# Another bank for the second layer behind a switch, and case numbers loaded one block ahead

## The chip, the cores and the metric

The kernel runs on one core of a Trainium2 chip. The metric is the time of one execution in microseconds (us) on the device, as the median of several runs. PE is the matrix engine (TensorE), PEld its weight loads, DVE the vector engine, ACT the scalar engine, POOL GpSimd and SP the engine that starts most transfers. A name with a q behind it (PEldq, DVEq, ACTq, POOLq) is the instruction queue of that engine, where register, branch and semaphore instructions run.

## The reference, cut to what matters

An attention with a window and some global rows makes 8 x 544 = 4352 rows of 512 numbers. Each row then goes through one of 8 experts, chosen by a gate that may keep the expert of the row before:

```python
def _moe_ref(x, w_gate, w_local, w1, w2):
    ...
            e = fresh_e if s == 0 or local_gate[b, s] < 0.5 else prev_e
            ...
            h = np.maximum(x[b, s] @ w1[e], 0.0)
            out[b, s] = p[e] * (h @ w2[e])
```

w1 is 8 x 512 x 1024 and w2 is 8 x 1024 x 512, all in 32-bit floats. How many rows each expert gets is known only when the kernel runs.

## The kernel before, in words

Until about 290 us the attention fills PE, and the rows that it makes go to a table `xs` in device memory. Then follow the experts, in blocks of up to 512 rows of one expert. Each matrix product is taken as three, with every operand split into a rounded high part and a low rest (`hi`, `lo`; `XH`, `XL` for the rows; `HH`, `HL` for the hidden layer).

`run` goes through `block(i)`:

- i = 0 to 2 are "early" blocks of 256 rows (`early`), during which the lists of the rows are still being made.
- i = 3 to 10 are "rem" blocks, one per expert, of a number of rows that is known only at run time. The text counts them as rem 1 to rem 8. A `tc.Switch` over `NCASE` = 34 cases picks the code ("arm") by a case number, `self.cv[k]`, a register on each engine, loaded from the tile `cnd` by `bound`. Case 0 is `half` (few rows, with the operands of the first layer exchanged), the others are `part` with another width of the row tile.
- i = 11 and up are "full" blocks of 256 rows under nested `tc.If`; three of them run with this input.

The chip has 8 banks of PSUM, `ps[0]` to `ps[7]`, each 128 x 512 numbers. In a `part`, the first layer makes 8 column blocks (`fc` = 0 to 7). Each is 12 matmuls into one bank (`mm1`, L1282), and the banks are taken in the order 2, 3, 6, 1, 7, 2, 3, 6. ACT reads a bank through a relu into `HH` (L1284), and DVE makes `HL` (L1287). Then comes the second layer (`mm2`, L1295; `thin`, L1301), 24 matmuls for 128 rows into a bank: ps0 or ps1 (`self.py.t`), or ps7 for the last part of a rem block.

The 128 rows with the number 2 (`REM`), the middle rows, are in every arm, and their second layer comes once behind the switch, where the arms join: `close(i, REM)`. `close` first stores ps7, then runs 24 matmuls, then stores that bank too. `store` is an ACT instruction that scales the bank into a tile `y` (L1313) and an indirect transfer on POOL that scatters `y` to the output (L1314).

Just ahead of `close`, `hint(i + 1)` loads the case number of the next block (`bound`, a TENSOR_LOAD of L1495 on each engine) and gives each engine the hint where the next switch will go (L1501: a few register instructions and a BRANCH_PREFETCH_HINT). For the first rem block this stands in `early(2)`, at `fc == 4` of the second layer.

Around this run three streams of preparation. Weights: SP loads raw tiles, ACT rounds them (`split`, L1174), and DVE makes the rest (L1184). Rows: POOL gathers the rows of block i + 2 (`gather`, L1215, four transfers per rem block). PE turns the rows of block i + 1 (`xpose`, L1236), and ACT and DVE copy the bank (L1238, L1239). In a `part` the four turns lie between second-layer matmuls, and the gather is issued behind the last. In `half` the turns and the gather stand at the end of the arm, where PE has little else to do.

The order on each engine is that of the code. A tile is guarded by semaphores that the framework sets from what uses it. Where a switch's arms join, the waits behind it count from the end of whichever arm ran, so one wait stands for all arms, and each arm is padded to the same counts.

## Time and profile before

| | us |
|---|---|
| median of three runs (lowest, highest) | 681.4 (680.08, 683.91) |
| profiled execution | 683.3 |
| its span | 681.6 |
| PE busy in it | 653.2 (96%) |
| DVE busy | 432.4 (63%) |
| ACT busy | 342.0 (50%) |
| POOL busy | 189.5 (28%) |

The mean granted clock of PE is 0.998. The profiled execution is 1.9 us above the median of the runs, and its span leaves out 1.7 us around it.

A row of the timeline has the start, the length, the engine, the line and operation, the tile written, the tile read, and the count of instructions that were put together; in brackets stands how long the engine was idle before it, and what ended that ("issue" means that no wait shows). Tiles bear the name of the buffer as it was allotted, so a piece of a weight may be called `wp`, `xh`, `hh` or `xa`.

The widths of the first layer's matmuls tell which arm ran: rem 1 has 456 columns, rem 2 is `half`, then 352, 440, 344, 288, 440 and 408 columns in rem 3 to rem 8. Their first layers begin at 321.8, 365.5, 382.4, 417.8, 459.3, 494.9, 524.5 and 566.0 us; the first full block begins at 605.0 us.

### The profile page before, as it was taken

What the parts mean: (1) busy time and instruction counts of PE and PEld (TensorE: products, weight loads), DVE (VectorE), ACT (ScalarE), POOL (GpSimd) and SP (SyncE); (2) the same over time, 40 slices, a digit from 0 to 9 for tenths busy, and PEclk for the clock granted to TensorE, in tenths of its full rate; (3) what the DMA queues carried; (4) which work ended last, traced back from release to release, by engine and by line L of the source; (5) the groups of instructions that cost most, each with busy time, mean ns of one, the idle gap of its engine ahead of it and who ended that gap; (6) DMA issues with size and microseconds to landing.
All of it is one profiled execution on the core that took longest, in us unless ns stands there. A gap on an engine that the chain in (4) does not pass through costs nothing.

```text
span 681.6 us, 18538 instructions
## 1 busy us (share of the span) xinstructions
PE 653.2 (96%) x7285; PEld 554.9 (81%) x7285; DVE 432.4 (63%) x1099; ACT 342.0 (50%) x612; POOL 189.5 (28%) x321
## 2 busy tenths in 40 slices
PE   8999999999999899998999899999999999999996
PEld 7778778777677787886988887989798989898994
DVE  7878788788887677987424653535353525355663
ACT  4555556554555674643426634344444435255563
POOL 7634344243334301031121303030303020212012
PEclk9999999999999999999999999999999999999999
DMA  8956958866857497766636566437474636355683
GB/s 326 406 211 251 346 202 321 317 236 238 296 200 288 144 330 276 262 201 205 250 116 223 196 235 204 155 117 224 139 226 115 212 117 202 131 184 185 225 269 107
DMA packets 42882, 151.42 MB, mean 222 GB/s; under 512 B 7838, under 2 KB 9118, under 8 KB 38561
## 3 DMA queue, kind: packets, MB, share of 16 engines
q1 hardware_dynamic: 35536, 126.92, 52.5%
q0 software_dynamic: 6832, 21.90, 9.9%
q8 instruction: 77, 1.26, 0.7%
q14 instruction: 149, 1.21, 0.6%
q10 hardware_dynamic: 288, 0.13, 0.1%
HBM read 130.55 MB, written 19.16 MB: 220 GB/s over the span
## 4 chain that ended last, share of the span: by engine, by line
PE 56%; DVE 5%; issue 2%; ACT 1%; POOL 1%; DVEq 0%; POOLq 0%; ACTq 0%
PE ps L1282 27%; PE ps L1295 23%; PE ps L1236 2%; PE ps L1301 2%; DVE wq L1184 1%; DVE wp L1184 1%; PE ps L1421 1%; DVE xT L1003 0%; ACT wp L1238 0%; POOL out_dram L1314 0%; DVE xT L1001 0%; PE ps L1011 0%; ACT wp L1174 0%; DVE o L917 0%; DVE xl L1239 0%
## 5 line engine op out<-in xcount | busy, mean ns | idle before, releaser
L1295 PE MATMUL ps<-wp,wq 128*128 128x512 f32 x444 | 111.3, 398 | 2.8 <-ACT wp L1238 2.8
L1282 PE MATMUL ps<-wp,wp 128*128 128x256 f32 (+6 forms) x672 | 108.0, 320 | 1.5 <-issue 1.5
L1282 PEld LDWEIGHTS ps<-wp,wp 128*128 128x128 f32 x672 | 103.2, 188 | 5.9 <-issue 2.7
L1215 POOL DMA_INDIRECT xa<-xs,idx x42 | 41.7, 992 | 209.6 <-PE ps L1295 103.1
L1295 PEld LDWEIGHTS ps<-wp,wq 128*128 128x128 f32 x444 | 81.5, 188 | 20.0 <-ACT wp L1238 3.1
L1287 DVE SCALAR_TENSOR_TENSOR wq<-ps,wq 128x384 fp32r<-128x384 f32 (+4 forms) x112 | 42.8, 412 | 64.6 <-ACT wq L1284 56.7
L1314 POOL DMA_INDIRECT out_dram<-y,tk x39 | 43.3, 1109 | 124.9 <-ACT y L1313 80.2
L194 POOL TENSOR_SCALAR_AFFINE_SELECT qbd<-raw 64x512 f32<-64x512 f32 x62 | 44.5, 718 | 116.9 <-PE ps L247 96.3
L1184 DVE TENSOR_TENSOR wp<-raw,wp 128x1024 fp32r<-128x1024 f32 x47 | 56.8, 1217 | 24.6 <-ACT wp L1174 18.3
L1284 ACT ACTIVATE wq<-ps 128x256 fp32r<-128x256 f32 (+6 forms) x80 | 36.6, 465 | 71.3 <-PE ps L1282 63.9
L247 PE MATMUL ps<-kx,qbd 128*64 128x128 f32 x1024 | 67.3, 274 | 1.5 <-issue 1.0
L258 ACT ACTIVATE pe<-pe 128x512 f32<-128x512 f32 x64 | 40.7, 636 | 44.0 <-DVE pe L254 44.0
L247 PEld LDWEIGHTS ps<-kx,qbd 128*64 128x64 f32 x1024 | 58.4, 138 | 2.3 <-issue 1.2
L1313 ACT ACTIVATE y<-ps,pp 128x512 f32<-128x512 f32 x35 | 24.2, 691 | 70.1 <-PE ps L1295 49.7
L252 DVE TENSOR_REDUCE mx<-ps 128x4 f32<-128x512 f32 x64 | 43.8, 685 | 23.8 <-PE ps L247 23.6
L1174 ACT CAST wp<-raw 128x1024 fp32r<-128x1024 f32 x49 | 50.5, 1048 | 1.3 <-ACT hh L1284 0.5
L1238 ACT CAST wp<-ps 128x512 fp32r<-128x512 f32 x40 | 23.4, 590 | 47.4 <-PE ps L1236 46.1
L1239 DVE TENSOR_TENSOR wp<-ps,wp 128x512 fp32r<-128x512 f32 x40 | 27.5, 691 | 29.3 <-ACT wp L1238 29.1
L254 DVE TENSOR_TENSOR pe<-ps,mx 128x512 f32<-128x512 f32 x64 | 44.0, 687 | 1.6
L280 PEld LDWEIGHTS ps<-v,pt 128*32 128x32 f32 x2048 | 32.9, 110 | 14.0 <-issue 8.3
L194 POOL TENSOR_SCALAR_AFFINE_SELECT kx<-raw 128x384 f32<-128x384 f32 (+3 forms) x127 | 42.9, 372 | 2.7 <-DMA raw<-in_qk_dram 0.5
L280 PE MATMUL ps<-v,pt 128*32 128x65 f32 x2048 | 41.4, 222 | 2.1 <-DVE xa L288 0.7
(302 smaller groups left out, 1185.6 us busy)
## 6 DMA issues: line engine op xcount, KB each, us to landing
raw<-in_w_dram SPq DMA_DIRECT2D x78, 512.0 KB, 3.7
v<-in_vw_dram SPq DMA_DIRECT2D x32, 1040.0 KB, 7.5
raw<-in_qk_dram SPq DMA_DIRECT2D x32, 528.0 KB, 8.0
xa<-in_w_dram SPq DMA_DIRECT2D x26, 512.0 KB, 4.3
xT<-in_w_dram SPq DMA_DIRECT2D x20, 512.0 KB, 5.5
xs<-xa SPq DMA_DIRECT2D x8, 1056.0 KB, 6.1
qgb<-in_qg_dram SPq DMA_DIRECT2D x8, 128.0 KB, 4.5
xa<-xs,idx POOLq DMA_INDIRECT x42
```

The lines of the kernel that those rows point to most:

```text
L194: self.nc.gpsimd.affine_select(out=out, in_=in_, pattern=pat, compare_op=ALU.is_ge, fill=0.0, base=0, channel_multiplier=0)
L247: nc.tensor.matmul(sp[64 * t2:64 * t2 + 64, t], qbd[:, w], kf[:, f:f + P], start=False, stop=True, skip_group_check=True)
L252: nc.vector.tensor_reduce(out=mx, in_=st["sp"], axis=AX.X, op=ALU.max)
L254: nc.vector.tensor_tensor(out=st["pe"][:, 4 * hb:4 * hb + 4], in0=st["sp"], in1=mx.broadcast_to([P, 4, P]), op=ALU.subtract)
L280: nc.tensor.matmul(o[32 * w4:32 * w4 + 32, g, h], pt[:, 2 * g + w4 // 2, w4 % 2, h, :], v[:, w, h * (D + 1):(h + 1) * (D + 1)], start=True ...
L1174: nc.scalar.copy(out=hi, in_=raw)
L1184: (nc.gpsimd if pool else nc.vector).tensor_tensor(out=lo, in0=raw, in1=hi.bitcast(F32), op=ALU.subtract)
L1215: self.nc.gpsimd.indirect_dma_start(out=self.xr[j] if k == "early" else self.xr4[:, j], out_offset=None, in_=src, in_offset=bass.IndirectO ...
L1282: nc.tensor.matmul(ph, a[:, dc, fs], b_[:, dc, n0:n1], start=(n == 0), stop=(n == 11))
L1287: nc.vector.scalar_tensor_tensor(out=o[:, fc, c:c + b_ - a], in0=ph[:, a - n0:b_ - n0], scalar=0.0, in1=hh[:, fc, a:b_].bitcast(F32), op0= ...
L1295: nc.tensor.matmul(py, a[:, fc, js], b_[:, fs], start=(fc == 0 and k == 0), stop=(fc == 7 and k == 2))
L1314: sc = nc.gpsimd.indirect_dma_start(out=self.out, out_offset=bass.IndirectOffsetOnAxis(ap=tk[rows, js], axis=0), in_=y[rows], in_offset=No ...
```

## The change

Two edits.

The bank. For a rem block `close` uses `ps[6]` in place of ps0 (`self.py.t[0]`). In `half` the four banks of the first layer are taken as 2, 3, 1, 6 in place of 2, 3, 6, 1, and the last turn goes into `ps[0]` in place of `ps[6]`.

The case number. A new function `ahead(i + 2)` stands right behind `hint(i + 1)`, in `early(2)` and behind each switch. It loads the case number of the block after next, so that at the next hint the number is in the register and no load stands ahead of it. Behind the hint for rem 8 it loads the number for the `If` of the full blocks, which was loaded ahead of the first `If`. In `early(2)` stand two loads now, one ahead of the hint and one behind it.

```diff
@@ early
                 self.hint(i + 1)
+                self.ahead(i + 2)
@@ half
-            ph = ps[(2, 3, 6, 1)[k]][:, 0:256]
+            ph = ps[(2, 3, 1, 6)[k]][:, 0:256]
...
-        self.xpose(i + 1, 3, ps[6])
+        self.xpose(i + 1, 3, ps[0])
@@ close
-        py = self.py.t[j % 2]
+        py = self.ps[6] if self.kind(i) == "rem" else self.py.t[j % 2]
@@ new, behind bound
+    def ahead(self, i):
+        if self.kind(i) == "rem":
+            self.bound(1 + i - NX, NCASE - 1)
+        else:
+            self.bound(0, NR)
@@ block, behind the switch
             self.hint(i + 1)
+            self.ahead(i + 2)
             self.close(i, REM)
```

The rows of PE where the arms of the first switch join, before. Names are tile and number of use: `cnd_298` is the tile of case numbers, `ps0_63` bank 0, `wp6` a piece of the second layer's weights, `wq0` and `wq1` are `HH` and `HL`. `Activation_49` and `DVE_49` are the semaphores that ACT and DVE raise.

```order
L1625 UNCONDITIONAL_BRANCH
L1495 TENSOR_LOAD cnd_298
L1501 SWITCH_STRIDE
L1501 ISA
L1501 BRANCH_PREFETCH_HINT
L1295 MATMUL ps0_63<-wp6_4376,wq0_4378 128x512 [waits Activation_49]
L1295 MATMUL ps0_63<-wp6_4376,wq0_4378 128x512
L1295 MATMUL ps0_63<-wp6_4376,wq1_4379 128x512 [waits DVE_49]
```

The same place now (L1496 is the load, L1508 the hint):

```order
L1633 UNCONDITIONAL_BRANCH
L1508 SWITCH_STRIDE
L1508 ISA
L1508 BRANCH_PREFETCH_HINT
L1496 TENSOR_LOAD cnd_298
L1295 MATMUL ps6_69<-wp6_4376,wq0_4378 128x512 [waits DVE_49,Activation_49]
L1295 MATMUL ps6_69<-wp6_4376,wq0_4378 128x512
L1295 MATMUL ps6_69<-wp6_4376,wq1_4379 128x512
```

The load has changed places with the hint, the second layer writes bank 6, and its first matmul carries the wait for DVE that the third had; the other joins read alike.

The rows of PE in the first layer of a rem block, in the arm with 440 columns of the second switch, before: the second, third and fourth column block. `wp4` and `wp5` are the high and low rows, `hl` and `wp0` pieces of the weights.

```order
L1282 MATMUL ps3_66<-wp4_4273,hl_91 128x440 x8
L1282 MATMUL ps3_66<-wp5_4375,hl_91 128x440 x4
L1282 MATMUL ps6_69<-wp4_4273,wp0_100 128x440 x4
L1282 MATMUL ps6_69<-wp4_4273,wp0_100 128x440 [waits DVE_49]
L1282 MATMUL ps6_69<-wp4_4273,wp0_100 128x440 x3
L1282 MATMUL ps6_69<-wp5_4375,wp0_100 128x440 x4
```

And now:

```order
L1282 MATMUL ps3_66<-wp4_4273,hl_91 128x440 x8
L1282 MATMUL ps3_66<-wp5_4375,hl_91 128x440 x4
L1282 MATMUL ps6_69<-wp4_4273,wp0_100 128x440 [waits Activation_49]
L1282 MATMUL ps6_69<-wp4_4273,wp0_100 128x440 x3
L1282 MATMUL ps6_69<-wp4_4273,wp0_100 128x440 [waits DVE_49]
L1282 MATMUL ps6_69<-wp4_4273,wp0_100 128x440 x3
L1282 MATMUL ps6_69<-wp5_4375,wp0_100 128x440 x4
```

The third column block, which takes bank 6, now begins with a wait for ACT; what it waits for is the store (L1313) of the `close` before, which reads that bank.

## The prediction

> **What bounds the kernel now.** The first part of the page comes first:

> ```profile
> span 681.6 us, 18538 instructions
> PE 653.2 (96%) x7285; PEld 554.9 (81%) x7285; DVE 432.4 (63%) x1099; ACT 342.0 (50%) x612; POOL 189.5 (28%) x321
> L1295 PE MATMUL ps<-wp,wq 128*128 128x512 f32 x444 | 111.3, 398 | 2.8 <-ACT wp L1238 2.8
> L1282 PE MATMUL ps<-wp,wp 128*128 128x256 f32 (+6 forms) x672 | 108.0, 320 | 1.5 <-issue 1.5
> ```

> PE is busy 96% of the span. The change takes no matmul away and adds none, so it can only move PE's idle time. The waits of PE from 290 us on, where the experts run (total, times, longest):

> ```profile
> PE ps L1282 <- issue: 3.1, 2, 1.6
> PE ps L1295 <- ACT wp L1238: 2.8, 1, 2.8
> PE ps L1236 <- DVE wp L1239: 2.2, 1, 2.2
> PE ps L1282 <- DVE hl L1287: 1.6, 1, 1.6
> PE ps L1295 <- ACT wp L1174: 0.7, 1, 0.7
> ```

> Together 10.4 us. The first row is two switches, the second the join behind the half arm, the third early block 2. These three lie where the change works; all of them taken away would be 8.1 us, 1.2% of the time. What the change can add must be a new wait, so I went to the timeline at each join.

> **The join behind the half arm (rem 2).** Rows of the timeline of ACT, DVE, PE and POOL there:

> ```profile
> 373.22 1.07 ACT L1174 CAST hh<-raw 128x1024 fp32r<-128x1024 f32 x1
> ...
> 374.81 0.69 DVE L1239 TENSOR_TENSOR wp<-ps,wp 128x512 fp32r<-128x512 f32 x1 [0.52 <-ACT wp L1238]
> ...
> 375.59 1.10 ACT L1238 CAST wp<-ps 128x512 fp32r<-128x512 f32 x2
> ...
> 376.74 4.40 PE L1295 MATMUL ps<-wp,wq 128*128 128x512 f32 x18 [2.82 <-ACT wp L1238]
> ...
> 378.81 1.33 POOL L1215 DMA_INDIRECT xa<-xs,idx  x1 [11.16 <-PE ps L1295]
> ...
> 382.35 4.01 PE L1282 MATMUL ps<-wp,hh 128*128 128x352 f32 x24
> ...
> 384.94 0.69 ACT L1313 ACTIVATE y<-ps,pp 128x512 f32<-128x512 f32 x1 [2.93 <-DMA xa<-xs,idx]
> ...
> 386.19 4.01 PE L1282 MATMUL ps<-wp,hl 128*128 128x352 f32 x24
> ```

> Now the second layer waits for ACT's last two copies of turned rows, which end at 375.59 + 1.10 = 376.69. With bank 6 the count that it needs of DVE and ACT is an earlier one: by the order of the two engines' instructions, the subtraction at 374.81, which ends at 375.50, and the cast at 373.22, which has long ended. PE's last copy at 376.74 started 0.05 behind its release, so it would start at 375.55: 1.19 us earlier.

> The third column block of rem 3 stands at 386.19 and would come to 385.00. It takes bank 6 and now waits for the store that empties it: 384.94 + 0.69 = 385.63. That store doesn't move, as it waits for the gather issued at 378.81, 6.1 us before, which is on POOL and depends on the turns that the change leaves in place. With the same 0.05, PE starts at 385.68 instead of 386.19. Net -0.5 us of the 1.2. The price is between -1.2 (the store is done in time) and +0.6 (the second layer starts no earlier, the wait comes anyway); -0.5 is the value that the rows themselves give.

> **The other joins.** Every rem block and the first full block get the same new wait at the third column block, 24 matmuls behind the end of `close`. Behind rem 6:

> ```profile
> 524.49 14.65 PE L1282 MATMUL ps<-wp,wp 128*128 128x440 f32 x72
> ```

> ```profile
> 525.06 1.14 POOL L1215 DMA_INDIRECT xa<-xs,idx  x1 [0.30 <-issue]
> ...
> 531.54 0.69 ACT L1313 ACTIVATE y<-ps,pp 128x512 f32<-128x512 f32 x1 [4.77 <-issue]
> ```

> ```profile
> L1313 ACTq EVENT_SEMAPHORE  x5: 17/38/8808, 522.2 to 531.5; - x5
> ```

> The first row is PE in rem 7, the next two POOL's last gather and ACT's store, the fourth the store's waits in ACT's queue from 520 to 535 us (least, median and greatest, in ns). Rem 7 takes bank 6 at 524.49 + 24 x 14.65 / 72 = 529.37. ACT's store of the second layer stands in the queue for 8.8 us, behind the gather issued at 525.06, and ends at 531.54 + 0.69 = 532.23. Nobody waits for it before, as bank 0 isn't needed until the second layer of rem 7. Bank 6 is: PE would stop for 532.23 + 0.05 - 529.37 = 2.9 us. Nothing hides this; behind it PE is as full as before. It is zero if the gather lands 2.9 us earlier, and grows with each us that it lands later. I take 2.9.

> The other stores end in time. The closest is the first full block, PE and then ACT:

> ```profile
> 604.97 7.30 PE L1282 MATMUL ps<-wp,wp 128*128 128x256 f32 x60
> ```

> ```profile
> 605.22 0.69 ACT L1313 ACTIVATE y<-ps,pp 128x512 f32<-128x512 f32 x1 [1.04 <-issue]
> ```

> Bank 6 is wanted at 604.97 + 24 x 7.30 / 60 = 607.89, the store ends at 605.91: 2.0 us to spare, cost 0.

> **The hint without a load ahead of it.** The two gaps at switches (rem 4 and rem 6), and PE's queue at them: the compare and branch of the switch (L1625), and the load and the hint at the join:

> ```profile
> 417.83 1.06 PE L1282 MATMUL ps<-wp,xh 128*128 128x440 f32 x4 [1.59 <-issue]
> ...
> 494.86 6.61 PE L1282 MATMUL ps<-wp,wp 128*128 128x288 f32 x48 [1.53 <-issue]
> ```

> ```profile
> L1625 PEldq COMPARE_BRANCH x2: 303/2870/5438, 406.5 to 412.2; - x2
> ...
> L1495 PEldq TENSOR_LOAD <-cnd x1: 314/314/314, 406.8 to 406.8; - x1
> ...
> L1501 PEldq MOVE x3: 29/29/34, 407.3 to 407.6; - x3
> ...
> L1501 PEldq BRANCH_PREFETCH_HINT x1: 40/40/40, 407.8 to 407.8; - x1
> ...
> L1625 PEldq COMPARE_BRANCH x1: 5077/5077/5077, 489.5 to 489.5; - x1
> ```

> The branch at 412.2 takes 5.4 us until the arm's code is there; the queue of matmuls ahead of it covers all but 1.6 us. The hint is given 4.4 us ahead of the branch. The load begins at 406.8 and the hint's first move at 407.3. Without the load, the hint stands some 0.4 us earlier (0.31 of load, 0.1 behind it). If the code arrives a fixed time behind the hint, each gap shrinks by 0.4: -0.8 for both. The bounds are 0, where the fetch begins at the branch, and -3.1 (1.59 + 1.53), where an earlier hint gets ahead of other fetches. I take -0.8, nearest to the one row with a duration, the load. At the other switches PE shows no gap, so nothing is to be won there. The load now lies behind the hint, ahead of the second layer's first matmul in PE's queue; the queue runs ahead of PE (the hint of rem 4 at 407.8, the arm at 417.83), so this is hidden but behind the half arm, where PE waits for DVE longer than that.

> [...]

> **Early block 2.** Two loads now, one ahead of the hint and one behind. The chain of waits, DVE's load there, and PE's wait:

> ```profile
> 310.90 0.33 DVEq L1495
> ...
> 311.71 0.06 DVEq L1501
> 311.77 0.17 issue
> 311.94 0.61 DVE xT L1001
> ...
> 317.83 0.04 issue
> 317.88 0.66 PE ps L1236 x4
> ```

> The chain goes through DVE's queue: load, hint, then DVE's next instruction at 311.94, and DVE full until PE gets its bank at 317.88. A second load of 0.31 us behind the hint starts DVE 0.3 us later, and so PE. The bounds: 0 (the 0.17 and the 1.2 us instruction that runs on DVE then hide it) to +0.45 (load and the step behind it). I take +0.3. On PE, ACT and POOL the second load delays at most what ends before PE's wait of 2.2 us, which absorbs it. In all there are 9 loads per engine before and after; the one ahead of the first `If` moves to an earlier join, where PE's queue runs ahead, cost 0.

> **The sum.** +0.3 (early block 2) - 0.5 (half arm with rem 3) - 0.8 (two switches) + 2.9 (rem 7) = +1.9 us, on the profiled execution's 683.3. That execution stands 1.9 us above the median of the runs, 681.4; the change should add the same to the median: 683.3 us.

> **The rivals.**

> [...]

> *The hint does nothing.* The change then doesn't do what it says for the switch: 0 instead of -0.8, sum +2.7, 684.1 us. For it: the same 4.4 us that bought nothing visible.

> *The stores come in time.* The gathers land earlier than in this execution or the store waits for less than the trace shows, so neither rem 7 nor rem 3 stops: +0.3 - 1.2 - 0.8 = -1.7, 679.7 us. Against it: 6.1 and 6.5 us from issue to the store in two places. If both gaps went too: -4.0, 677.4 us.

> *The other side: the gathers land later.* The wait in rem 7 and that in rem 3 are both set by a gather, so each us by which gathers land later costs up to 2 us. The sum passes 3.4 us (0.5%, about what a measurement of this kernel can tell from no change) when they land 0.8 us later, 7.1 instead of 6.3. At 1.5 us later the sum is 1.9 + 3.0 = +4.9, 686.3 us. For it: the transfers are dense in that stretch. Windows: between, busy times of PE, PEld, DVE, ACT, POOL, granted clock, DMA share, GB/s:

> ```profile
> 373.90:376.70 2.80, 0.03 (x1) 0.00 (x0) 2.28 (x4) 2.80 (x6) 0.00 (x0) 1.00 0.03 13
> 376.70:382.50 5.80, 5.76 (x25) 4.77 (x26) 4.01 (x8) 5.31 (x6) 3.08 (x3) 1.00 0.67 224
> 529.40:532.30 2.90, 2.90 (x16) 2.73 (x15) 0.15 (x1) 0.69 (x1) 0.00 (x0) 1.00 0.87 282
> ```

> Against it: nothing in the change moves POOL's gathers or SP's transfers.

> *The clock falls in the new stall.* If the stop of 2.9 us in rem 7 brought the granted clock to half for as long again as it lasts, the work in these 2.9 us would lose half of them, 1.5 us: sum +3.4, 684.8 us. Against it: in 2.8 us of idle PE, the first two windows, the clock stayed at 1.00, and 2.9 is hardly more. [...]

> **How the numbers follow.** Forecast as summed, 0.45. Hint does nothing, 0.17. Hint overtakes, 0.13. Stores in time, 0.10, a third of it with both gaps gone. Gathers later, 0.11. Clock, 0.04. "Slower by over 0.5%" is the last two less the cases of a small delay, and the error of two medians (the three runs spread over 3.8 us): 0.14. "Faster" is the third of "stores in time" and that error: 0.06. The rest, 0.80, is within 0.5%. The likeliest case is 683.3 us; the range goes from "stores in time", 679.7, to "gathers later", 686.3.

> **What would show it.** In the profile after: PE L1282 waits for ACT y L1313 twice, 2.9 us at about 531 and 0.6 at about 385; PE L1295 behind the half arm is idle for 1.6 instead of 2.8, ended by DVE wp L1239; the issue gaps at rem 4 and rem 6 are 1.2 and 1.1; PE's wait in early block 2 is 2.5 instead of 2.2. Gaps of 1.6 again say that the hint has no part in the fetch, none at all that it leads it. No wait for L1313 would put my reading of the new wait wrong, and with it the sign of the sum.

## The result, and the profile after

The changed kernel takes 686.6 us (median of 9 runs, 685.5 to 689.5) against 681.9 us of the kernel before (9 runs beside them, 680.1 to 685.8). The ratio is 1.0067 with a 95% interval of 1.0047 to 1.0088: slower by 0.7%, 4.7 us, where 1.9 us were forecast. It lies 0.3 us above the forecast's range.

The profiled execution took 688.3 us. First part of its page:

```profile
span 686.6 us, 18548 instructions
PE 657.2 (96%) x7285; PEld 557.8 (81%) x7285; DVE 432.9 (63%) x1099; ACT 342.1 (50%) x612; POOL 190.9 (28%) x321
L1282 PE MATMUL ps<-wp,wp 128*128 128x256 f32 (+6 forms) x672 | 111.0, 326 | 3.6 <-ACT y L1313 3.5
```

The same 672 first-layer matmuls keep PE busy for 111.0 us instead of 108.0: 326 ns each instead of 320. Something has made equal work slower, besides the idle time. PE's waits from 290 us on:

```profile
PE ps L1282 <- ACT y L1313: 3.5, 1, 3.5
PE ps L1236 <- DVE wp L1239: 2.1, 1, 2.1
PE ps L1295 <- DVE wp L1239: 1.7, 1, 1.7
PE ps L1282 <- DVE hl L1287: 1.7, 1, 1.7
PE ps L1295 <- issue: 1.0, 1, 1.0
PE ps L1282 <- ACT wp L1174: 0.8, 1, 0.8
PE ps L1282 <- issue: 0.3, 1, 0.3
```

The first row is the new wait, once and not twice. The 2.8 us behind the half arm are 1.7, ended by DVE. The two gaps "issue" at switches are one of 0.3. PE's timeline and POOL's last gather and ACT's store in rem 7:

```profile
522.43 5.08 PE L1282 MATMUL ps<-wp,wp 128*128 128x440 f32 x24
...
531.02 4.40 PE L1282 MATMUL ps<-wp,wp 128*128 128x440 f32 x11 [3.51 <-ACT y L1313]
```

```profile
523.01 1.66 POOL L1215 DMA_INDIRECT xa<-xs,idx  x1 [0.30 <-issue]
...
530.28 0.69 ACT L1313 ACTIVATE y<-ps,pp 128x512 f32<-128x512 f32 x1 [5.42 <-issue]
```

PE stops after 24 matmuls until ACT has stored bank 6. Behind the stop 11 matmuls take 4.40 us, 0.40 each, where 24 took 5.08, 0.21 each. Windows around it, and around early block 2 (start and end, length, busy times of five engines, granted clock, DMA share, GB/s):

```profile
314.80:317.30 2.50, 0.37 (x2) 0.00 (x0) 2.46 (x5) 0.30 (x1) 0.00 (x0) 1.00 0.62 193
317.40:322.00 4.60, 4.60 (x31) 3.81 (x32) 2.16 (x6) 1.86 (x3) 0.24 (x1) 0.63 0.53 144
527.40:531.00 3.60, 0.11 (x1) 0.00 (x0) 0.15 (x1) 0.69 (x1) 0.00 (x0) 0.90 0.93 289
531.00:537.10 6.10, 6.08 (x17) 5.49 (x18) 2.15 (x4) 2.72 (x5) 1.00 (x1) 0.50 0.34 133
```

After the stop PE runs at half its clock for over 6 us. It also does for a while in early block 2, behind an idle time of only 2.1 us that stood in the profile before too (2.2 us) and left the clock at 1.00 there.

Both traces have the same 7285 matmuls, so the start of the same one in both tells where the time went:

| PE at | before | after | difference | step |
|---|---|---|---|---|
| third turn in early block 2 | 317.88 | 317.31 | -0.57 | differences ahead of the experts |
| first matmul of rem 1 | 321.81 | 322.84 | +1.03 | +1.60 half clock |
| second layer behind the half arm | 376.74 | 376.68 | -0.06 | -1.09 shorter wait |
| rem 3 | 382.35 | 383.24 | +0.89 | +0.95 branch of the switch ended late |
| rem 4 | 417.83 | 417.54 | -0.29 | -1.18 gap 1.59 to 0.32 |
| rem 6 | 494.86 | 492.89 | -1.98 | -1.69 gap 1.53 to 0 |
| rem 7 | 524.49 | 522.43 | -2.06 | -0.08 |
| third column block of rem 7 | 529.38 | 531.02 | +1.64 | +3.70 stop |
| sixth column block of rem 7 | 536.58 | 541.08 | +4.50 | +2.86 half clock |
| rem 8 | 565.97 | 570.70 | +4.73 | +0.23 |

Two of these rows, rem 4 and rem 6, are gains; whether they come from the change is a question for the experiments.

### The profile page after: what moved, and what is told of

Read it like the earlier page. It is cut to its first block, busy times and chain, and to the rows that moved or that the text cites. A ratio compares the mean times of both kernels' runs of the same rounds, so it can differ in the third digit from the quotient of the medians.

```text
span 686.6 us, 18548 instructions
## 1 busy us (share of the span) xinstructions
PE 657.2 (96%) x7285; PEld 557.8 (81%) x7285; DVE 432.9 (63%) x1099; ACT 342.1 (50%) x612; POOL 190.9 (28%) x321
## 4 chain that ended last, share of the span: by engine, by line
PE 51%; DVE 5%; DMA 3%; issue 3%; ACT 2%; POOL 1%; DVEq 0%; POOLq 0%; ACTq 0%
PE ps L1282 26%; PE ps L1295 19%; DMA out_dram<-y,tk 3%; PE ps L1236 2%; PE ps L1301 2%; DVE wq L1184 1%; DVE wp L1184 1%; ACT wp L1174 1%; POOL out_dram L1314 1%; POOL xa L1215 1%; PE ps L1011 0%; DVE xT L1003 0%; DVE xT L1001 0%; DVE o L917 0%; DVE xl L1239 0%
## 5 line engine op out<-in xcount | busy, mean ns | idle before, releaser
L1282 PE MATMUL ps<-wp,wp 128*128 128x256 f32 (+6 forms) x672 | 111.0, 326 | 3.6 <-ACT y L1313 3.5
L1295 PE MATMUL ps<-wp,wq 128*128 128x512 f32 x444 | 111.3, 397 | 1.7 <-DVE wp L1239 1.7
L1282 PEld LDWEIGHTS ps<-wp,wp 128*128 128x128 f32 x672 | 105.6, 192 | 8.5 <-ACT y L1313 3.9
L1215 POOL DMA_INDIRECT xa<-xs,idx x42 | 42.7, 1017 | 215.2 <-PE ps L1295 102.7
L1295 PEld LDWEIGHTS ps<-wp,wq 128*128 128x128 f32 x444 | 81.5, 188 | 18.9 <-ACT wp L1238 1.9
L1287 DVE SCALAR_TENSOR_TENSOR wq<-ps,wq 128x384 fp32r<-128x384 f32 (+4 forms) x112 | 42.9, 413 | 70.3 <-ACT wq L1284 63.9
L1313 ACT ACTIVATE y<-ps,pp 128x512 f32<-128x512 f32 x35 | 24.2, 691 | 67.8 <-PE ps L1295 54.4
L1174 ACT CAST wp<-raw 128x1024 fp32r<-128x1024 f32 x49 | 50.6, 1050 | 2.1 <-DVE wp L1184 1.3
L1238 ACT CAST wp<-ps 128x512 fp32r<-128x512 f32 x40 | 23.5, 590 | 47.7 <-PE ps L1236 46.3
L1239 DVE TENSOR_TENSOR wp<-ps,wp 128x512 fp32r<-128x512 f32 x40 | 27.5, 691 | 29.6 <-ACT wp L1238 29.4
```

Source lines behind the costliest of these rows:

```text
L1174: nc.scalar.copy(out=hi, in_=raw)
L1215: self.nc.gpsimd.indirect_dma_start(out=self.xr[j] if k == "early" else self.xr4[:, j], out_offset=None, in_=src, in_offset=bass.IndirectO ...
L1282: nc.tensor.matmul(ph, a[:, dc, fs], b_[:, dc, n0:n1], start=(n == 0), stop=(n == 11))
L1287: nc.vector.scalar_tensor_tensor(out=o[:, fc, c:c + b_ - a], in0=ph[:, a - n0:b_ - n0], scalar=0.0, in1=hh[:, fc, a:b_].bitcast(F32), op0= ...
L1295: nc.tensor.matmul(py, a[:, fc, js], b_[:, fs], start=(fc == 0 and k == 0), stop=(fc == 7 and k == 2))
```

## The experiments

All ran five rounds, interleaved with the kernel before; a ratio is to the kernel before on the same chip, with its 95% interval.

**The bank edit alone, the loads alone.** Without `ahead`:

```diff
-                self.ahead(i + 2)
-            self.ahead(i + 2)
```

> The bank edit alone: second layer into bank 6, the case number loaded ahead of the hint as before. Theory S (the stop in rem 7 and the half clock behind it cost 3.5 + 2.9 us, and the earlier hint pays 2.7 us back at the switches of rem 4 and rem 6): the stop stays and the payment goes, so slower than the changed kernel, 6 to 7 us above the kernel before (688 to 689), with gaps of about 1.5 us at those two switches and a granted clock near 0.5 for some microseconds behind the stop in rem 7. Rival L (the loss comes from the loads: two in early block 2, and shifted code): close to the kernel before, within 2 us.

Measured: 686.6 us, ratio 1.0061 (1.0038 to 1.0083). The other half of the change by itself, from the changed kernel:

```diff
-        py = self.ps[6] if self.kind(i) == "rem" else self.py.t[j % 2]
+        py = self.py.t[j % 2]
-            ph = ps[(2, 3, 1, 6)[k]][:, 0:256]
+            ph = ps[(2, 3, 6, 1)[k]][:, 0:256]
-        self.xpose(i + 1, 3, ps[0])
+        self.xpose(i + 1, 3, ps[6])
```

> The loads one block ahead alone, second layer in bank 0 as before. Theory S: no stop in rem 7, no fall of the clock there, gaps at rem 4 and rem 6 gone or under 0.5 us: 2 to 3 us faster than the kernel before (679 to 680). Rival L: 3 to 5 us slower than before, like the changed kernel. Rival N (the gaps vanished by chance in one execution): same as before within 1 us, with gaps of 1.5 us back.

Measured: 683.1 us, ratio 0.9997 (0.9981 to 1.0013). The loss is the bank edit's; the loads neither cost nor bring over 0.2%. Rival L falls, and so does the half of theory S by which the earlier hint pays 2.7 us back: without it the bank edit costs as much as with it. Rival N is borne out: the loads alone take the time of the kernel before. PE of the bank edit alone in rem 7, and the windows there:

```profile
530.51 11.41 PE L1282 MATMUL ps<-wp,wp 128*128 128x440 f32 x48 [3.63 <-ACT y L1313]
```

```profile
526.90:530.50 3.60, 0.00 (x0) 0.00 (x0) 0.15 (x1) 0.69 (x1) 0.00 (x0) 1.00 0.93 316
530.60:534.80 4.20, 4.20 (x14) 3.82 (x15) 1.41 (x3) 1.95 (x4) 1.00 (x1) 0.59 0.35 134
```

The stop is there again, and the clock falls again behind it, for about half as long.

**The stop taken away in two ways.** Bank 6 later in the first layer of every part:

```diff
-            self.mm1(..., self.ps[(2, 3, 6, 1, 7, 2, 3, 6)[fc]], few if thin else 0)
+            self.mm1(..., self.ps[(2, 3, 1, 7, 6, 2, 3, 1)[fc]], few if thin else 0)
```

> The changed kernel with the first layer of a part taking its banks in the order 2, 3, 1, 7, 6, 2, 3, 1, so that bank 6 is wanted 24 matmuls later. Theory S: the store has ended by then (4.9 us later at 440 columns against a stop of 3.5), no stop and no fall of the clock in rem 7: 6 us faster than the changed kernel, 680 to 681. Rival L: no better than the changed kernel, 686 to 687.

Measured: 680.2 us, ratio 0.9962 (0.9940 to 0.9985). Taking the stop away makes a kernel that is faster than before. The waits of PE in rem 7 (515 to 545 us) now have no store among them, but a smaller one of DVE, whose work follows ACT's. That the late store, which still holds ACT up, is the cause is argued, not shown:

```profile
PE ps L1282 <- DVE wq L1287: 0.9, 1, 0.9
```

The late order did more than take the stop away. In this trace the second layer behind the half arm runs on without any wait, where the changed kernel waits for 1.7 us, and in rem 3 PE waits for DVE for 1.6 us. This order wasn't run on the kernel before, so what it is worth by itself isn't known. PE behind the half arm:

```profile
375.26 4.37 PE L1295 MATMUL ps<-wp,wq 128*128 128x512 f32 x18
```

The other way is to let the store go earlier: an output tile of its own, here the attention's idle tile `gsb`.

```diff
+    def store(self, py, j, thin=False, y=None):
+        y = self.y() if y is None else y
...
+        self.store(py, j, y=self.yc if self.kind(i) == "rem" else None)
...
+    moe.yc = at.gsb
```

> The changed kernel with an output tile of its own for the store of the second layer behind the switch (an idle tile of the attention), so that ACT's store doesn't wait for transfers that share a semaphore with the gathers. If the store is late because of these transfers, it runs right behind the second layer (about 1 us behind the end of the arm), PE doesn't stop in rem 7, the clock stays at 1.00: 680 to 681. If the store is late because of ACT's own casts or of the bank, it stays late and the time stays at 686 to 687.

Measured: 684.9 us, ratio 1.0045 (1.0025 to 1.0065): neither value. The stop in rem 7 was gone, but this tile is also one that the half arm writes, and PE there waited for it:

```profile
372.30 0.71 PE L1410 MATMUL ps<-idf,gsb 128*128 128x128 f32 x4 [2.44 <-ACT gsb L1425]
```

So the time of this run doesn't tell what the store is worth. The same with a tile that the half arm doesn't touch (against the run just shown):

```diff
-    moe.yc = at.gsb
+    moe.yc = moe.xr[0][:, 0:DM]
```

> The changed kernel with an output tile of its own for the store behind the switch, this time one that the half arm doesn't write (the early blocks' row tile). If the store was late only because its output tile waits for transfers: no stop in rem 7 over 1 us, no fall of the clock there, and no wait in the half arm: 680 to 681. If not: 684 and above.

Measured: 680.5 us, ratio 0.9960 (0.9942 to 0.9978). ACT's row of the store, and the window of rem 7 in which PE had stopped:

```profile
523.87 0.69 ACT L1313 ACTIVATE xr<-ps,pp 128x512 f32<-128x512 f32 x1
```

```profile
526.00:532.00 6.00, 6.00 (x31) 5.63 (x30) 3.01 (x7) 3.51 (x6) 0.99 (x1) 1.00 0.89 297
```

The store runs right behind ACT's casts, 2.5 us behind the start of rem 7 (523.87 against 521.34), where it came 7.9 us behind it (530.28 against 522.43), and PE runs through. So the store was late because of its output tile, which comes from a ring whose last use lies in the arm: the wait for the transfers that emptied the ring ends only when the last gather has landed. By the profile that gather takes 7.0 us from issue to landing in the changed kernel (523.01 + 7.0 = 530.0) and 7.1 us with the bank edit alone (522.41 + 7.1 = 529.5); the store begins 0.3 us behind that in both, at 530.28 and 529.77. The profile's times for the last gather alone, in the changed kernel and with the bank edit alone:

```profile
DMA to landing us min/median/max: 7.0/7.0/7.0
DMA to landing us min/median/max: 7.1/7.1/7.1
```

The two remedies come to the same time within their intervals, 7 us under the changed kernel. Each has something of its own besides the stop: the late order the shorter wait behind the half arm, the own tile 0.2% on the kernel before (1.6 us, last experiment). With that taken off, 7.3 - 1.6 = 5.7 us are left for the stop and what follows it. That is the whole loss of 4.7 us, and probably more; the intervals, 1.2 to 1.4 us to each side, don't settle how much more.

**The clock's share.** PE is kept busy during the stop, in rem 7 alone:

```diff
+            if i == 9 and fc == 2:
+                w = self.wp[8 * i][0].rearrange("p (c f) -> p c f", c=4)
+                for m in range(12):
+                    self.nc.tensor.matmul(self.ps[0][:, 0:n1 - n0], w[:, 0, 0:P], x[0][:, 0, n0:n1], start=True, stop=True)
```

> The changed kernel, and in rem 7 twelve matmuls of no use (the arm's width, 440 columns here, into bank 0, which nobody reads) ahead of the third column block, where PE stops. They take 12 x 0.203 = 2.4 us of the stop of 3.5 us. Theory S: the third column block starts when it did (the store sets it), PE is idle for 1.1 us only, the clock stays at 1.00 in rem 7, and the time falls by what the clock cost there, 1.5 us per 3.4 us at half speed: 684 to 685.5. If the clock doesn't fall because of the idle time, or its fall costs nothing: 686.6 as the changed kernel.

Measured: 685.5 us, ratio 1.0032 (1.0014 to 1.0050). PE in rem 7, and the windows of the filled part, the idle part and behind them:

```profile
527.96 2.57 PE L1456 MATMUL ps<-wp,wp 128*128 128x440 f32 x12
532.31 9.88 PE L1282 MATMUL ps<-wp,wp 128*128 128x440 f32 x48 [1.78 <-ACT y L1313]
```

```profile
527.96:530.50 2.54, 2.54 (x13) 2.07 (x11) 0.00 (x0) 0.00 (x0) 0.00 (x0) 1.00 0.98 214
530.50:532.30 1.80, 0.03 (x1) 0.00 (x0) 0.15 (x1) 0.69 (x1) 0.00 (x0) 1.00 1.01 410
532.30:538.00 5.70, 5.69 (x28) 5.35 (x29) 2.95 (x6) 3.52 (x6) 1.00 (x1) 1.00 0.31 122
```

The useful work is held up for 4.35 us here (2.57 and 1.78), longer than the 3.51 of the changed kernel, and the clock stays at 1.00. The ratio falls by 0.0035, 2.4 us; the intervals of the two ratios overlap a little, so the size is rough. It goes the way of the clock: the mean granted clock was 0.9933 over 9 executions of the changed kernel and 0.9964 over 12 of this one, so (0.0031 x 686) / 0.5 = 4.3 us less at half speed, worth 2.1 us of work, less the 0.8 us by which the useful work is held up longer.

**Short idle times.** The same idea at the two places where PE always stands idle for about 2 us, on the kernel with the second own tile (`warm` writes matmuls of no use into a free bank):

```diff
+                if fc == XPM[2]:
+                    self.warm(i, self.ps[2], 7)
                 self.xpose(i + 1, XPM.index(fc))
...
+        self.warm(i, self.ps[1], 5)
         self.scals(i + 1)
```

> The changed kernel with the output tile of its own, and matmuls of no use where PE stands idle for about 2 us: seven of 512 columns ahead of the third turn in early block 2, five at the end of the half arm. If an idle time of 1.7 to 2.8 us lets the clock fall in some executions (half speed for 3.4 us, 1.5 us each), the mean granted clock rises from 0.9964 to 0.998 and the time falls by about 1 us: 679 to 680, and the executions lie closer together. If such idle times have no part in it: 680.5, clock 0.996.

Measured: 681.2 us, ratio 0.9970 (0.9955 to 0.9985), mean clock 0.9973 against 0.9964 without the fillers. The clock moved as expected, the time didn't: a miss, or a gain too small to see (0.0009 of 681 us is 0.6 us). That the clock falls behind such idle times in some executions is in the traces (the changed kernel in early block 2, above; the loads alone behind the half arm):

```profile
375.30 6.01 PE L1295 MATMUL ps<-wp,wq 128*128 128x512 f32 x18 [2.82 <-ACT wp L1238]
```

```profile
376.60:380.60 4.00, 4.00 (x12) 3.17 (x11) 2.37 (x3) 4.00 (x5) 2.62 (x3) 0.57 0.71 239
```

The same wait of 2.82 us left the clock at 1.00 in the execution that the prediction read.

Why it falls in some executions and not in others can be read from the traces. Each fall of the clock that has work behind it lasts 3.41 us, once twice that, and in a trace with several they begin whole multiples of 3.413 us apart: 318.62 and 530.25 in the changed kernel, 62 times; 318.78, 329.02 and 387.05 without the hint, 3 and 17 times. So in these traces the clock changes on a raster of 3.41 us. Stretches of that raster, in the changed kernel, then in the loads alone, then in the kernel before (its raster is taken from the fall at 678.75, behind its last matmul):

```profile
315.21:318.62 3.41, 1.30 (x9) 1.14 (x10) 2.65 (x4) 0.59 (x1) 0.00 (x0) 1.00 0.72 198
318.62:322.03 3.41, 3.41 (x25) 2.79 (x24) 1.70 (x5) 1.27 (x2) 0.27 (x1) 0.50 0.42 126
526.83:530.25 3.42, 0.68 (x4) 0.29 (x2) 0.15 (x1) 0.00 (x0) 0.18 (x1) 1.00 0.91 259
530.25:533.66 3.41, 2.64 (x7) 2.42 (x8) 0.00 (x0) 0.69 (x1) 1.00 (x1) 0.50 0.81 321
533.66:537.07 3.41, 3.41 (x11) 3.04 (x11) 2.12 (x4) 2.69 (x5) 0.00 (x0) 0.50 0.03 10
```

```profile
373.41:376.82 3.41, 1.52 (x7) 1.25 (x8) 3.41 (x8) 3.41 (x6) 0.00 (x0) 1.00 0.22 44
376.82:380.24 3.42, 3.42 (x10) 2.68 (x9) 2.15 (x2) 3.42 (x4) 2.30 (x2) 0.50 0.65 213
```

```profile
371.55:374.96 3.41, 2.38 (x22) 2.13 (x20) 2.04 (x4) 3.36 (x7) 0.00 (x0) 1.00 0.66 234
374.96:378.37 3.41, 1.63 (x7) 1.36 (x8) 3.41 (x8) 3.41 (x6) 0.00 (x0) 1.00 0.22 54
```

What goes with a fall here is how much PE works in one stretch: 1.30, 0.68 and 1.52 us ahead of the three falls. In the kernel before the same 2.82 us of idle time lie across a border, with 2.38 and 1.63 us of work in the two stretches, and nothing falls. The 13 kept traces that have a fall to lay the raster by fit, from 296 us to the stretch of PE's last matmul: at full clock a fall followed each stretch with up to 1.3 us of work (10 times), three of eight with 1.5 to 1.74 us, and none with more. So what an idle time of 2 to 3 us did in these traces was a matter of where it fell on the raster.

**What the hint does.** Three kernels. The late bank without the earlier hint:

```diff
-                self.ahead(i + 2)
-            self.ahead(i + 2)
-            self.mm1(..., self.ps[(2, 3, 6, 1, 7, 2, 3, 6)[fc]], few if thin else 0)
+            self.mm1(..., self.ps[(2, 3, 1, 7, 6, 2, 3, 1)[fc]], few if thin else 0)
```

> The bank edit with the first layer's banks in the order 2, 3, 1, 7, 6, 2, 3, 1, and the case number loaded ahead of the hint as before: the kernel of the late bank without the earlier hint. If the earlier hint is worth what its 0.42 us give at two or three switches (0.8 to 1.5 us): 681 to 682. If it is worth nothing, as the loads alone would have it: 680.2, as the late bank with it.

Measured: 680.8 us, ratio 0.9962 (0.9946 to 0.9978), the same as with the earlier hint. Then the kernel before with a later hint:

```diff
-            self.hint(i + 1)
             self.close(i, REM)
@@ close
         for fc in range(8):
+            if fc == 1 and self.kind(i) == "rem":
+                self.hint(i + 1)
             self.mm2(i, py, fc, j, self.HH, self.HL)
```

> The kernel before, with load and hint moved behind the first three matmuls of the second layer behind the switch (on ACT behind the store of bank 7). If the arm's code comes a fixed time behind the hint (8.3 us on the mean so far, while the branch comes 4.5 us behind it), the gaps at rem 4 and rem 6 grow by as much as the hint is later, and others open: slower than before by 1 to 4 us. If the hint has no part in the fetch: the gaps stay at 0.5 to 1.6 us and the time within 1 us of before.

Measured: 683.8 us, ratio 1.0004 (0.9991 to 1.0017). And without any:

```diff
-            self.tc.switch_hint({e: self.cv[k] for e in ENGS}, NCASE, label=f"rem{k}")
...
-            for case in self.tc.Switch(self.cv[k], NCASE, hint=f"rem{k}"):
+            for case in self.tc.Switch(self.cv[k], NCASE):
```

> The kernel before without the hint (the load stays). If the hint starts the fetch of the arm, the code comes later at every switch: 2 us or more per rem block, slower by over 5 us. If the fetch of PE's arm begins with the branch or with the code ahead of it whatever the hint says: within 1 us of before, and the code still comes 8 to 11 us behind the branch to the join.

Measured: 690.8 us, ratio 1.0100 (1.0072 to 1.0128). That looks as if the hint mattered everywhere, but the trace puts the loss in one place, the first switch: 5.2 us of idle PE and one stretch at half clock behind it (329.02 to 332.44). PE at rem 1 and the branch in its queue, without the hint and then in the kernel before:

```profile
329.00 1.50 PE L1282 MATMUL ps<-wp,wp 128*128 128x456 f32 x3 [5.22 <-issue]
```

```profile
L1624 PEldq COMPARE_BRANCH  x1: 5788/5788/5788, 323.1 to 323.1; - x1
```

```profile
L1625 PEldq COMPARE_BRANCH  x1: 342/342/342, 321.3 to 321.3; - x1
```

Behind the joins the picture is another. The time from the start of PE's branch to a join (a COMPARE_BRANCH in its queue) to the end of the COMPARE_BRANCH of the next switch, in us, from each trace (that the branch ends when the arm's code is there is the author's reading, no view shows an arm's fetch):

| kernel | hint | rem 3 | rem 4 | rem 5 | rem 6 | rem 7 | rem 8 |
|---|---|---|---|---|---|---|---|
| before | load ahead of it | 7.9 | 11.2 | 9.1 | 11.2 | 8.8 | 9.6 |
| bank alone | load ahead of it | 9.9 | 10.4 | 9.2 | 10.2 | 8.7 | 9.8 |
| late bank, no `ahead` | load ahead of it | 9.0 | 10.1 | 9.3 | 7.1 | 8.5 | 9.1 |
| changed | no load ahead | 10.0 | 9.9 | 9.1 | 7.9 | 8.8 | 9.8 |
| loads alone | no load ahead | 8.3 | 8.3 | 9.9 | 11.0 | 8.2 | 9.2 |
| late bank | no load ahead | 7.4 | 10.0 | 9.5 | 7.8 | 8.2 | 9.6 |
| second own tile | no load ahead | 9.8 | 9.2 | 9.1 | 7.6 | 8.6 | 9.4 |
| hint late | behind 3 matmuls | 10.7 | 8.3 | 9.1 | 10.3 | 8.2 | 9.5 |
| no hint | none | 10.8 | 10.7 | 9.2 | 9.9 | 8.8 | 9.6 |

In rem 5, 7 and 8 the branch ends at the same time, within 0.8 us, with an early, a late and no hint. In rem 3, 4 and 6 it ends 7.1 to 8.3 or 9.0 to 11.2 us behind the branch to the join, in the five kept traces that the table leaves out too; without a hint (one execution) only the longer times are there, with one both, in any of its places. The gaps of 1.59 and 1.53 us of the kernel before are its two 11.2; the changed kernel's -1.2 at rem 4 is most likely the draw of one execution, as longer and shorter times are there with either bank. At two switches the bank may have a part. In rem 3 the time is 9.5 to 10.0 in all six kept traces in which `close` and the third column block share bank 6, and 7.9 to 8.3 in the three with bank 0 and the hint in its place. In rem 6 the shorter time is there in six of nine traces with bank 6 and in none of five with bank 0. Why these three have two values isn't settled, nor whether 0.4 us of earlier hint makes the shorter one likelier; in time it is under 0.2% either way.

**Own tile on the kernel before, and both remedies.** The own tile alone (bank 0, loads as before):

```diff
-        self.store(py, j)
+        self.store(py, j, y=self.yc if self.kind(i) == "rem" else None)
...
+    moe.yc = moe.xr[0][:, 0:DM]
```

`store` takes `y` as above.

> The kernel before (bank 0, loads as before) with the output tile of its own for the store behind the switch, nothing else. If the own tile is worth something without the bank edit (ACT comes to the next arm earlier): faster than before by 1 us or so, and the bank edit's own gain is what the changed kernel with the own tile has more. If it only mends the stop of the bank edit: same as before within 0.5 us.

Measured: 682.4 us, ratio 0.9977 (0.9956 to 0.9998). The own tile has some worth by itself. The kernel with the bank edit, the loads and the own tile stands at 0.9960, so what the change has left without its stop is 0.2%, inside the intervals. Own tile and later bank together, against the run with `gsb`:

```diff
-            self.mm1(..., self.ps[(2, 3, 6, 1, 7, 2, 3, 6)[fc]], few if thin else 0)
+            self.mm1(..., self.ps[(2, 3, 1, 7, 6, 2, 3, 1)[fc]], few if thin else 0)
-    moe.yc = at.gsb
+    moe.yc = moe.xr[0][:, 0:DM]
```

> The changed kernel with both remedies: bank 6 wanted 24 matmuls later in the first layer, and an output tile of its own for the store. If each only takes away the same stop, the two together are worth what one is: 680 to 680.8. If the later bank still had a cost of its own (ACT held back by the late store, which let PE wait for DVE in rem 3 and rem 7): under 680.

Measured: 680.4 us, ratio 0.9949 (0.9928 to 0.9971). It is faster than both kernels; against either remedy alone the intervals overlap.

## Why the prediction was wrong, point by point

*The new wait in rem 7 (+2.9)*: right in place, cause and sign, and shown by the two remedies. It was 3.5 us. PE wanted the bank 5.1 us behind the start of rem 7, where 4.9 were worked out; but the store began 7.3 us behind the issue of the last gather (523.01 to 530.28) where the prediction had 6.5 from one execution. That is the rival of the later gathers, 0.8 us later, at the low end of what it named.

*The clock behind it (0, with 0.04 for a fall)*: the step that failed most. The prediction took two windows of one execution, 2.8 us of idle PE at a clock of 1.00, as a bound below which nothing falls, and a stop of 2.9 as hardly more. That it didn't fall there was luck: the 2.8 us lay across two stretches of the raster, with 2.38 and 1.63 us of work. In other executions the same 2.8 us made the clock fall, and the stop was longer. The profile before has a longer idle time too, behind PE's last matmul, which ends at 674.93, and the clock is at 0.50 there from 678.75 on. The rival that named the fall had the mechanism, at 1.5 us and a chance of 0.04. That the half clock lasts as long as the stop, from which its 1.5 us come, no run shows: it lasted 6.83 us behind a stop of 3.51 us in the changed kernel and 3.41 us behind one of 3.63 with the bank edit alone. With the fall, the term is 3.7 + 2.9 = 6.6 us by the two profiled executions, in place of 2.9, and 5.7 to 7.3 us by the ratios with and without the stop, the lower one with the own tile's 0.2% taken off. Over all executions the clock's part is smaller than the 2.9 of the profiled one: the mean clock is 0.9933 in the changed kernel and 0.9967 and 0.9964 with the two remedies, 0.0031 to 0.0034 of 686 us, 2.1 to 2.3 us.

*The half arm (-1.2, net -0.5)*: the second layer began 1.1 us earlier, as worked out, ended by the DVE instruction that was named. The wait for the store in rem 3 that was to take 0.6 of it back didn't come; instead the branch of the switch ended late, which the prediction didn't have. The trace's releaser "ACT wp L1174" is misleading there, PE's own queue shows it:

```profile
383.24 1.05 PE L1282 MATMUL ps<-wp,hh 128*128 128x352 f32 x5 [0.80 <-ACT wp L1174]
```

```profile
L1633 PEldq COMPARE_BRANCH  x1: 4300/4300/4300, 378.7 to 378.7; - x1
```

The branch of the switch takes 4.30 us and ends at 383.0, 10.0 us behind the branch to the join instead of 7.9 (first column of the table). Net -0.1 us in this execution. The term lacks the clock: behind the 2.8 to 2.9 us of the kernels with bank 0 it fell in three of five kept traces, behind the 1.7 to 1.8 us of those with bank 6 in none of four. At 1.7 us for each fall (half of 3.41) that would be a gain of about 1 us on the mean, an estimate from few traces.

*The hint (-0.8)*: the step "the code arrives a fixed time behind the hint" failed. Behind a join the branch ends at a time that the hint moves little or not at all (within 0.8 us in rem 5, 7 and 8), and the two gaps from which the term was made belong to the two longest times of the table, 11.2 us. The rival "the hint does nothing" was the nearest in mechanism, with 0.17; only the first switch contradicts it (342 ns with the hint, 5788 without). The chance of 0.13 for "hint overtakes" belongs to the bound of -3.1; no run shows fetches that a hint gets ahead of, and the loads alone took 0.9997 of the time of the kernel before, with two gaps of 1.6 us together at switches.

*Early block 2 (+0.3)*: no cost seen. PE's wait was 2.14 us, before 2.21, and the loads alone cost nothing in time. That is the lower bound, 0.

The sum, with what was measured: 0 - 0.1 + 0 + 6.6 = 6.5 us for the causes that the runs bear out, less the 2.9 us at the switches of rem 4 and rem 6, plus the fall of the clock in early block 2, +1.6, less 0.6 ahead of the experts, plus 0.1 to 0.2 elsewhere, is the 4.7 us of the table. That the medians differ by 4.7 us too is chance: the fall in early block 2 comes or doesn't in any of these kernels (in five of the twelve kept traces with a wait of 2.1 to 2.3 us there). Over many executions such draws occur on both sides: over 26 executions of the kernel before the mean clock was 0.9946, while the profiled one that the prediction read had 0.998.

## What to carry to other kernels

When a buffer is exchanged for one that is wanted sooner, look for the instruction that empties it: a late store that nobody waited for becomes a stop of the engine that bounds the kernel, and the cure may be in the store's own wait (an output tile of its own) or in a later use of the bank. Price a new stop of PE with the clock behind it: here 1.7 us of work for each stretch of 3.41 us at half speed, one or two of them. One execution in which a short idle time left the clock alone is no bound, as the next can put the same idle time into one stretch of the raster. Don't make a term out of a gap that one trace shows at two of seven places: see first whether it is there in other executions.
